# Splitting the inputs of the wide products two f-tiles at a time, with the combinations spread evenly: a packed attention and two feed-forward layers on one Trainium2 core

## The chip, the core and the metric

The kernel runs on one core of one Trainium2 chip, in one launch. The metric is the device time in microseconds. Engines are TensorE (PE; its weight loads are PEld), VectorE (DVE), ScalarE (ACT), GpSimd (POOL) and SyncE (SP), which issues the DMAs. Each engine works through its own queue in order, and semaphores order the engines among each other.

## What is computed

Attention in two hops gives x of 4608 rows and 512 columns; two feed-forward layers follow, each with a 512 x 2048 and a 2048 x 512 matrix:

```python
p_packed = sm_attn(p, k, v)                  # 32 packed rows per head
out = sm_attn(q, p_packed, p_packed)         # 8 x 8 heads, 576 rows, 64 columns
x = out.transpose(0, 2, 1, 3).reshape(4608, 512)
h = x @ w_in;  x = np.maximum(0.01 * h, h) @ w_out            # first layer
h = x @ w_in2; out = (h * (1 / (1 + np.exp(-1.702 * h)))) @ w_out2   # second layer
```

## The kernel before

There are four stages: attention with the first layer's narrow product (matmuls of L338), the first wide product 2048 to 512 (L650, into `y`), the second layer's first product (L684, into `h`), and the second wide product (L762, into `sum`).

Matrices are multiplied in about fp32 accuracy from fp32r parts: an operand a is split into a high part (a cast on ScalarE, `nc.scalar.copy`) and a low part (a minus the high part, a subtraction on VectorE), and each product is three matmuls: high with high, high with low, low with high. The helper `split(step, high)` puts the cast into the agenda of one step and the subtraction (L107, `tensor_sub(*rest)`) into that of the next. `side(step)` then emits what a step's agenda holds, in the order in which it was entered, ahead of that step's matmuls (in the middle stage behind them).

The two wide products work in a Strassen-Winograd scheme: a block of 768 rows is cut into two halves of rows i and two halves of the 2048 inputs h, and seven products (order 1, 7, 5, 6, 2, 4, 3) of eight f-tiles each replace eight. A block so has 56 steps (`steps`), and there are six blocks. A step of L650 is six matmuls of 384 columns, one of L762 nine of 256. The inputs of the products are the raw tiles a11, a12, a21, a22 (tags r.., two f-tiles, 128 x 2 x 384, in each) or combinations of them, made in place by VectorE in `prepare`'s `combo`: S3 (L480, a11-a21) is read by product 7, S1 (L482, a21+a22) by product 5, S2 (L484, a22-a11) by product 6, S4 (L486, a12-a11) by product 3. After S4 the raw tile a11 of the next block is loaded; a21, a22 and a12 of the next block are loaded during products 5, 4 and 3. Loads wait in SP's queue until the readers of the old tile are done.

`high` (L492) splits one f-tile of step k: its cast is in the agenda of step k-3, the subtraction in that of k-2, into one of five rotating buffers (`ROLL, LEAD = 5, 2`). The tiles are called `ba` in the first wide product (raw `br`) and `da` in the second (raw `dr`). The matmuls of step k read both parts, and free the buffer for step k+5.

Other work shares the queues. In L650, `combined("wi2", ...)` converts the second layer's weights from 64-bit words: per piece a load into `raw_wi`, two casts on ScalarE (L121, L122), on VectorE a mask (L125) and a shift-or (L128), an integer add on GpSimd (L129, `b_wi`), then four small subtractions on VectorE (L144 to L148) three steps later. A piece that is loaded in step s is cast in s+14; pieces start at steps 26 and 44 of the first block, at 1, 19 and 38 of the next four, and at 1 and 19 of the last. Finished products are copied or added out of PSUM by `evacuate` (ScalarE for products 1, 7, 2, VectorE for 5, 6, 4, 3).

`y_block` prepares the inputs of the middle stage: for each of seven products it casts (L586) and subtracts (L107, `ya`) the two 128 x 384 halves at steps of their own, and its `combo` (L592, L593, L595, L597 on tiles `yq`) follows the second half. It runs for block 0 in the second half of the last block of L650, for block 1 at the start of the middle stage, for the others within it. There the weights `wj` are split too (cast L626, subtraction L107), and `unit` takes the sums out (`uv`, `cc`, L688 to L703).

Of the kernel before, what the change touches and what calls it, by code (L numbers as in the profile page):

```python
# [9 lines left out]
F32 = mybir.dt.float32  # L10
F32R = mybir.dt.float32r
# [10 lines left out]
P = 128  # L22
# [4 lines left out]
HB = TB // 2  # L27
# [12 lines left out]
PLACE = {1: (0, 0), 7: (0, 0), 5: (1, 0), 6: (0, 0), 2: (0, 1), 4: (1, 1), 3: (0, 1)}  # L40

COMBO = {1: 0, 2: 1, 3: 2, 5: 3, 7: 4, 6: 5, 4: 6}
EARLY = 5
ROLL, LEAD = 5, 2


def packed_attention_moe_moe_kernel(tc, qT, kT, vm, vt, pT, w_in1, w_out1, w_in2, w_out2, out):
# [4 lines left out]
    nc = tc.nc  # L52
# [13 lines left out]
    pools = {}  # L66
# [13 lines left out]
    with ExitStack() as ctx:  # L80
# [10 lines left out]
        def at(step, *todo):  # L91
            agenda.setdefault(step, []).extend(todo)
# [9 lines left out]
        def split(step, high):  # L102


            rest = []
            at(step, lambda: rest.extend(high()))
            at(step + 1, lambda: nc.vector.tensor_sub(*rest))  # L107
# [299 lines left out]
        for c in range(1, 4):  # L407
            for k in range(4):
                s = 8 * c - 8 + k
# [4 lines left out]
        for b in range(B):  # L414
            s = 32 * b
# [18 lines left out]
        wt, raws, ga, outs, early = {}, {}, {}, {}, {}  # L434
# [39 lines left out]
        def prepare(nm, g):  # L474


            def combo(blk, fp, what):
                a11, a12, a21, a22 = (raws.get((blk, i, h, fp)) for i in range(2) for h in range(2))
                if what == "S3":
                    nc.vector.tensor_sub(a11, a11, a21)  # L480
                elif what == "S1":
                    nc.vector.tensor_add(a21, a21, a22)  # L482
                elif what == "S2":
                    nc.vector.tensor_sub(a11, a22, a11)  # L484
                else:
                    nc.vector.tensor_sub(a12, a12, a11)  # L486
                    load_raw(blk + 1, 0, 0, fp, nm, g)

            def high(k, blk, p, f):
                src = raws[(blk, *PLACE[p], f // 2)][:, f % 2, :]  # L490
                t = ga[blk, p, f] = pools["dr"].tile([P, 2, HB], F32R, tag=f"s{k % ROLL}", name=f"{nm}a_{blk}_{p}_{f}")
                nc.scalar.copy(t[:, 0, :], src)  # L492
                return t[:, 1, :], src, t[:, 0, :].bitcast(F32)

            for blk in range(NBK):
                s = 7 * NJ * blk
                for what, when in (("S3", (1, 4, 7, 10)), ("S1", (12, 14, 16, 19)), ("S2", (20, 22, 24, 27)), ("S4", (34, 38, 42, 46))):
                    for fp, k in enumerate(when):
                        at(s + k, lambda blk=blk, fp=fp, what=what: combo(blk, fp, what))
            for k, step in enumerate(steps):  # L500
                split(k - LEAD - 1, lambda k=k, step=step: high(k, *step))
                blk, p, f = step
                if f % 2 and p in (5, 4, 3):
                    at(k - LEAD, lambda blk=blk, p=p, f=f: load_raw(blk + 1, *PLACE[p], f // 2, nm, g))

        def evacuate(k, blk, p, bank, shape, store):
            def tile_(what):
# [62 lines left out]
        def y_block(early, steps, blk):  # L570
# [7 lines left out]
                    q[i, j] = pools[home].tile([P, 2, HB], F32, tag=tag, name=f"yq_{blk}_{i}{j}")  # L578
                    nc.sync.dma_start(q[i, j], yT[2 * j:2 * j + 2, :, t0 + HB * i:t0 + HB * i + HB].rearrange("d p t -> p d t"))

            def one(p, k):
                src, i = q[PLACE[p]], PRODUCTS.index(p)
                if blk not in ya:
                    ya[blk] = pools["ABC"[blk % 3]].tile([P, 7, 2, 2, HB], F32R, tag="ABC"[blk % 3], name=f"ya_{blk}")
                t = ya[blk][:, i]
                nc.scalar.copy(t[:, 0, k], src[:, k])  # L586
                return t[:, 1, k], src[:, k], t[:, 0, k].bitcast(F32)

            def combo(p):
                sub = nc.vector.tensor_sub  # L590
# [6 lines left out]
                    sub(q[0, 1], q[0, 1], q[0, 0])  # L597
            at(early, load)
            for n, step in enumerate(steps):
                p, k = (1, 2, 7, 5, 6, 4, 3)[n // 2], n % 2  # L600
                split(step, lambda p=p, k=k: one(p, k))
                if k:
                    at(step + 1, lambda p=p: combo(p))

        PIECES = (slice(0, 2), slice(2, 4), slice(4, 6), slice(6, 7))
# [117 lines left out]
        for q in range(2):  # L723
            s = 14 * NJ * q
# [87 lines left out]
```

## Time and profile before

| | |
|---|---|
| runs | 1481.79 us median of 3 (1481.16 to 1482.88) |
| profiled execution | 1488.2 us, of it the profile's span 1486.4 us |
| mean granted TensorE clock | 0.98 |
| TensorE, VectorE, ScalarE, GpSimd busy | 95%, 75%, 56%, 7% of the span |
| L650, first wide product | 367.05 to 751.36 us |
| L684, middle stage | 751.36 to 1117.18 us |
| L762, second wide product | 1117.18 us to the end |

Times in the profile are microseconds from the span's start. A bracket at the end of a row says how long the engine had stood idle before it, and what ended the idle time. A matmul is counted busy while it is in the pipeline, so TensorE counts as busy also where its matmuls are slower than they could be.

### The profile page before, as it was taken

The page shows a single profiled execution, that of the slowest core. Times are in us where ns is not written, and L with a number is a line of the kernel's source. Part 1 is how long each engine was busy: PE and PEld are TensorE (multiplying, and loading weights), DVE is VectorE, ACT ScalarE, POOL GpSimd, SP SyncE. Part 2 cuts the span into 40 slices and gives each one's busy share as a digit, 9 for nine tenths or more (in the row PEclk, how much of TensorE's full clock was granted, in tenths as well). Part 3 has the DMA queues.
Part 4 walks back from the last instruction along what each step waited for, and adds up shares of the span by engine and source line. Part 5 has one row for each costly group of instructions (what it writes and reads, how often), then busy time and mean ns, then how long its engine had stood idle before and what let it go on. Part 6 is the DMA issues. An engine that isn't in the chain of part 4 may idle for free.

```text
span 1486.4 us, 27714 instructions
## 1 busy us (share of the span) xinstructions
PE 1417.2 (95%) x10400; PEld 1322.9 (89%) x10400; DVE 1107.5 (75%) x2068; ACT 836.2 (56%) x1791; POOL 100.4 (7%) x71
## 2 busy tenths in 40 slices
PE   6789999999979999999889999999999999999998
PEld 4567777778979999999789999999999999999998
DVE  5667777762859888888987887877648877777776
ACT  3656666665435545555656766666645655445443
POOL 1311110100001010110100010000000000000000
PEclk8889999999989999999999999999999999999999
DMA  9459999969993655635357786786768524515421
GB/s 365 159 194 318 308 325 307 335 212 337 325 301 118 212 187 164 223 105 197 120 184 249 250 282 238 244 276 204 242 216 276 170 88 148 181 54 170 129 85 43
DMA packets 228773, 317.42 MB, mean 214 GB/s; under 512 B 12576, under 2 KB 188704, under 8 KB 228640
## 3 DMA queue, kind: packets, MB, share of 16 engines
q1 hardware_dynamic: 228640, 315.67, 63.9%
q8 instruction: 81, 1.33, 0.4%
q14 instruction: 52, 0.43, 0.1%
HBM read 191.89 MB, written 123.73 MB: 212 GB/s over the span
## 4 chain that ended last, share of the span: by engine, by line
PE 71%; DVE 17%; issue 4%; DMA 3%; ACT 2%; POOL 2%; SPq 1%; DVEq 0%; ACTq 0%; POOLq 0%
PE sum L762 23%; PE h L684 20%; PE y L650 14%; PE h L338 10%; DVE ba L107 3%; PE m L218 2%; POOL b_wi L129 1%; PE pp L273 1%; PE s L218 1%; DVE m L327 1%; DVE br L482 1%; DVE br L484 1%; DVE wj L107 1%; DVE ya L107 1%; DVE da L107 1%
## 5 line engine op out<-in xcount | busy, mean ns | idle before, releaser
L684 PE MATMUL h<-ya,wj 128*128 128x384 f32 x2016 | 357.7, 338 | 6.7 <-DVE uv L692 2.4
L684 PEld LDWEIGHTS h<-ya,wj 128*128 128x128 f32 x2016 | 352.5, 189 | 11.7 <-DVE uv L692 4.1
L338 PEld LDWEIGHTS h<-a,m 128*128 128x128 f32 x1536 | 215.7, 195 | 53.7 <-ACT g L343 22.1
L650 PE MATMUL y<-ba,wo 128*128 128x384 f32 x1296 | 238.1, 341 | 19.6 <-DVE ba L107 10.9
L650 PEld LDWEIGHTS y<-ba,wo 128*128 128x128 f32 x1296 | 225.6, 189 | 31.2 <-DVE ba L107 22.4
L492 ACT CAST ba<-br 128x384 fp32r<-128x384 f32 x336 | 164.5, 513 | 149.7 <-PE y L650 89.8
L338 PE MATMUL h<-a,m 128*128 128x288 f32 x1536 | 239.5, 309 | 9.3 <-ACT a L315 3.5
L492 ACT CAST da<-dr 128x384 fp32r<-128x384 f32 x336 | 166.3, 514 | 145.2 <-PE sum L762 105.4
L762 PE MATMUL sum<-wo,da 128*128 128x256 f32 x1944 | 232.4, 281 | 1.6 <-DVE da L107 1.4
L762 PEld LDWEIGHTS sum<-wo,da 128*128 128x128 f32 x1944 | 230.2, 188 | 3.2 <-DVE da L107 3.2
L107 DVE TENSOR_TENSOR da<-dr,da 128x384 fp32r<-128x384 f32 x336 | 172.8, 554 | 40.5 <-ACT da L492 40.4
L107 DVE TENSOR_TENSOR ba<-br,ba 128x384 fp32r<-128x384 f32 x336 | 175.7, 556 | 25.5 <-ACT ba L492 25.5
L343 ACT ACTIVATE g<-h 128x288 f32<-128x288 f32 x256 | 105.2, 416 | 99.7 <-PE h L338 98.0
L762 PE MATMUL sum<-wo_early,da 128*128 128x256 f32 x1080 | 132.4, 285 | 1.7 <-ACT da L492 1.6
L762 PEld LDWEIGHTS sum<-wo_early,da 128*128 128x128 f32 x1080 | 131.5, 193 | 2.2 <-ACT da L492 1.9
L650 PE MATMUL y<-ba,wo_early 128*128 128x384 f32 x720 | 128.2, 340 | 2.3 <-ACT ba L492 2.2
L650 PEld LDWEIGHTS y<-ba,wo_early 128*128 128x128 f32 x720 | 126.4, 190 | 3.3 <-ACT ba L492 2.4
L327 DVE TENSOR_TENSOR m<-m,m 128x512 fp32r<-128x512 f32 x64 | 43.0, 684 | 54.6 <-ACT m L325 54.2
L129 POOL TENSOR_TENSOR b_wo<-v_wo,b_wo 128x512 int32<-128x512 int32 x32 | 42.5, 1330 | 485.5 <-DVE v_wo L128 367.6
L677 ACT ACTIVATE g<-cc 128x384 f32<-128x384 f32 x96 | 50.4, 525 | 31.6 <-DVE cc L700 27.1
L107 DVE TENSOR_TENSOR wj<-wjs,wj 128x512 fp32r<-128x512 f32 x88 | 55.8, 647 | 9.7 <-ACT wj L626 9.7
L692 DVE TENSOR_TENSOR uv<-uv,h 128x384 f32<-128x384 f32 x48 | 26.5, 553 | 46.5 <-PE h L684 39.9
(114 smaller groups left out, 1372.1 us busy)
## 6 DMA issues: line engine op xcount, KB each, us to landing
g_scratch<-g SPq DMA_DIRECT2D x64, 576.0 KB, 5.3
br<-g_scratch SPq DMA_DIRECT2D x96, 384.0 KB, 7.0
g_scratch<-g SPq DMA_DIRECT2D x96, 384.0 KB, 5.4
dr<-g_scratch SPq DMA_DIRECT2D x96, 384.0 KB, 4.3
wjs<-wi_scratch SPq DMA_DIRECT2D x22, 896.0 KB, 5.8
wo_scratch<-hl_wo SPq DMA_DIRECT2D x32, 448.0 KB, 6.0
wo<-wo_scratch SPq DMA_DIRECT2D x27, 512.0 KB, 8.9
k<-in_kT_dram SPq DMA_DIRECT2D x16, 576.0 KB, 6.3
```

The source lines that it names most:

```text
L107: at(step + 1, lambda: nc.vector.tensor_sub(*rest))
L129: nc.gpsimd.tensor_tensor(d, v.bitcast(I32), d, op=ALU.add)
L218: nc.tensor.matmul(tiles[par][32 * i:32 * i + 32, :n], lhsT=lhsT(r, i, par), rhs=rhs(r, i), start=True, stop=True)
L327: nc.vector.tensor_sub(m[:, 1, par, :], t[par], m[:, 0, par, :].bitcast(F32))
L338: nc.tensor.matmul(t[:, :TH], lhsT=m[:, ws, par, o:o + P], rhs=a[:, xs, par, :], start=(k == 0), stop=(k == 5))
L343: nc.scalar.activation(g1t[g][:, f % 2, hf * TH:hf * TH + TH], t[:, :TH], AF.Prelu, alpha=0.01)
L492: nc.scalar.copy(t[:, 0, :], src)
L650: nc.tensor.matmul(acc[BANK[p]][:, c, :HB], lhsT=w[:, ws, P * c:P * c + P], rhs=x[:, xs, :], start=(p in OPENS and f + m == 0), stop=(f == ...
L677: nc.scalar.activation(g[f][:, HB * i:HB * i + HB], src, AF.Gelu_apprx_sigmoid)
L684: nc.tensor.matmul(b, lhsT=w[:, ws, c, P * kk:P * kk + P], rhs=x[:, xs, kk, :], start=(p in OPENS and kk + s == 0), stop=(kk + s == 3), sk ...
L692: nc.vector.tensor_add(v, v, b)
L762: nc.tensor.matmul(b, lhsT=x[:, xs, P * c:P * c + P], rhs=w[:, ws, :], start=(p in OPENS and f == 0 and m == 0 and c != 1), stop=(f == NJ ...
```

## The change

In the wide products one cast and one subtraction now serve the two f-tiles of a raw tile (128 x 768 columns); the cast stands in the agenda of step k-4 (k even), the subtraction in k-3, and there are three buffers of a pair each in place of five of one f-tile. The steps of the combinations are S3 1, 3, 5, 7 (before 1, 4, 7, 10), S1 9, 11, 13, 15 (12, 14, 16, 19), S2 17, 19, 21, 23 (20, 22, 24, 27) and S4 36, 39, 41, 43 (34, 38, 42, 46). The loads of the next block keep their steps, but for those that follow S4. In `y_block` a product's two halves are cast and subtracted together at the step of the first one, and the combination follows one step after.

```diff
-ROLL, LEAD = 5, 2
+ROLL = 3
...
             def high(k, blk, p, f):
-                src = raws[(blk, *PLACE[p], f // 2)][:, f % 2, :]
-                t = ga[blk, p, f] = pools["dr"].tile([P, 2, HB], F32R, tag=f"s{k % ROLL}", name=f"{nm}a_{blk}_{p}_{f}")
-                nc.scalar.copy(t[:, 0, :], src)
-                return t[:, 1, :], src, t[:, 0, :].bitcast(F32)
+                src = raws[(blk, *PLACE[p], f // 2)]
+                t = pools["dr"].tile([P, 2, 2, HB], F32R, tag=f"s{k // 2 % ROLL}", name=f"{nm}a_{blk}_{p}_{f}")
+                for c in range(2):
+                    ga[blk, p, f + c] = t[:, :, c]
+                nc.scalar.copy(t[:, 0], src)
+                return t[:, 1], src, t[:, 0].bitcast(F32)
...
-                for what, when in (("S3", (1, 4, 7, 10)), ("S1", (12, 14, 16, 19)), ("S2", (20, 22, 24, 27)), ("S4", (34, 38, 42, 46))):
+                for what, when in (("S3", (1, 3, 5, 7)), ("S1", (9, 11, 13, 15)), ("S2", (17, 19, 21, 23)), ("S4", (36, 39, 41, 43))):
...
             for k, step in enumerate(steps):
-                split(k - LEAD - 1, lambda k=k, step=step: high(k, *step))
                 blk, p, f = step
-                if f % 2 and p in (5, 4, 3):
-                    at(k - LEAD, lambda blk=blk, p=p, f=f: load_raw(blk + 1, *PLACE[p], f // 2, nm, g))
+                if f % 2 == 0:
+                    split(k - 4, lambda k=k, step=step: high(k, *step))
+                elif p in (5, 4, 3):
+                    at(k - 2, lambda blk=blk, p=p, f=f: load_raw(blk + 1, *PLACE[p], f // 2, nm, g))
...
-            def one(p, k):
+            def one(p):
...
-                nc.scalar.copy(t[:, 0, k], src[:, k])
-                return t[:, 1, k], src[:, k], t[:, 0, k].bitcast(F32)
+                nc.scalar.copy(t[:, 0], src)
+                return t[:, 1], src, t[:, 0].bitcast(F32)
...
             for n, step in enumerate(steps):
-                p, k = (1, 2, 7, 5, 6, 4, 3)[n // 2], n % 2
-                split(step, lambda p=p, k=k: one(p, k))
-                if k:
+                if n % 2 == 0:
+                    p = (1, 2, 7, 5, 6, 4, 3)[n // 2]
+                    split(step, lambda p=p: one(p))
                     at(step + 1, lambda p=p: combo(p))
```

## Rows read from the trace of the kernel before

**Rows 1.** The page's busy times: us, share of the span, instructions

```profile
PE 1417.2 (95%) x10400; PEld 1322.9 (89%) x10400; DVE 1107.5 (75%) x2068; ACT 836.2 (56%) x1791; POOL 100.4 (7%) x71
```

**Rows 2.** Busy us (instructions) by stretch: PE, PEld, DVE, ACT, POOL; granted clock; DMA

```profile
367.05:439.70 72.65, 63.41 (x338) 62.11 (x339) 48.81 (x85) 31.76 (x65) 1.43 (x1) 0.91 1.00 335
...
421.70:425.90 4.20, 1.44 (x3) 1.04 (x4) 2.57 (x5) 3.25 (x7) 0.03 (x1) 0.50 1.01 369
...
562.46:623.34 60.88, 59.68 (x338) 58.08 (x337) 51.99 (x95) 32.80 (x65) 6.26 (x3) 1.00 0.55 175
...
684.24:751.36 67.12, 61.81 (x338) 57.64 (x337) 62.13 (x113) 37.26 (x77) 5.70 (x2) 1.00 0.32 100
...
1117.18:1180.97 63.79, 62.33 (x505) 61.52 (x506) 56.27 (x96) 39.56 (x80) 0.00 (x0) 0.97 0.75 250
1180.97:1240.88 59.91, 59.87 (x507) 59.67 (x506) 45.53 (x77) 29.85 (x59) 0.00 (x0) 1.00 0.42 133
```

**Rows 3.** The chain that ended last, in L650: start us, us, what

```profile
451.96 0.94 DVE ba L107 x2
452.90 0.87 DVE br L482
...
546.69 32.39 PE y L650 x185
```

**Rows 4.** Groups of instructions by form: busy us, mean ns, idle before

```profile
L107 DVE TENSOR_TENSOR ba<-br,ba 128x384 fp32r<-128x384 f32 x336 | 175.7, 556 | 25.5 <-ACT ba L492 25.5
...
L492 ACT CAST ba<-br 128x384 fp32r<-128x384 f32 x336 | 164.5, 513 | 149.7 <-PE y L650 89.8 <-DVE br L482 25.0 <-DVE br L484 21.1
...
L155 ACT CAST hl_wo<-b_wo 128x896 fp32r<-128x896 f32 x16 | 15.1, 945 | 8.9 <-DVE b_wo L148 8.6 <-issue 0.3
...
L315 ACT CAST a<-a 128x576 fp32r<-128x576 f32 x16 | 10.8, 674 | 7.6 <-DVE a L313 7.6
...
L128 DVE SCALAR_TENSOR_TENSOR v_wi<-v_wi,raw_wi 128x512 uint32<-128x512 uint32 x16 | 11.0, 685 | 0.0
...
L125 DVE TENSOR_SCALAR raw_wi<-raw_wi 128x512 uint32<-128x512 uint32 x16 | 6.8, 425 | 12.4 <-ACT v_wi L122 11.3 <-DMA br<-g_scratch 1.1
...
L513 ACT COPY v<-y 128x768 f32<-128x768 f32 x6 | 4.8, 798 | 2.5 <-PE y L650 2.5
...
L148 DVE TENSOR_TENSOR b_wi<-b_wi 128x128 f32<-128x128 f32 x16 | 4.7, 292 | 0.6
```

**Rows 5.** Timeline of VectorE and GpSimd in L650's fourth block: start us, us, what

```profile
581.89 2.05 DVE L482 TENSOR_TENSOR br<-br,br 128x768 f32<-128x768 f32 x1
...
603.22 3.29 POOL L129 TENSOR_TENSOR b_wi<-v_wi,b_wi 128x512 int32<-128x512 int32 x1 [20.10 <-DVE v_wi L128]
...
606.54 0.29 DVE L144 TENSOR_TENSOR b_wi<-b_wi 128x128 f32<-128x128 f32 x1 [1.18 <-POOL b_wi L129]
```

**Rows 6.** Timeline of TensorE in the same block

```profile
607.56 4.65 PE L650 MATMUL y<-ba,wo 128*128 128x384 f32 x25 [0.46 <-DVE ba L107]
```

**Rows 7.** Timeline of ScalarE and TensorE at the stop in the first block

```profile
422.09 0.66 ACT L121 ACTIVATE b_wi<-raw_wi 128x512 int32<-128x512 uint32 x1 [9.50 <-DMA raw_wi<-in_w_in_dram]
...
423.75 0.69 PE L650 MATMUL y<-ba,wo 128*128 128x384 f32 x1 [8.25 <-ACT ba L492]
```

**Rows 8.** Timeline of TensorE in the last block of L650

```profile
744.96 6.36 PE L650 MATMUL y<-ba,wo 128*128 128x384 f32 x35 [1.36 <-DVE ba L107]
```

**Rows 9.** Timeline of VectorE and TensorE at the start of L684

```profile
760.44 1.29 DVE L107 TENSOR_TENSOR wj<-wj 128x512 fp32r<-128x512 f32 x2
...
761.78 12.44 PE L684 MATMUL h<-ya,wj 128*128 128x384 f32 x68 [0.19 <-DVE wj L107]
...
762.23 0.96 DVE L592 TENSOR_TENSOR yq<-yq,yq 128x768 f32<-128x768 f32 x1
```

**Rows 10.** Timeline of VectorE and TensorE in L684, near 926 us

```profile
925.47 0.96 DVE L592 TENSOR_TENSOR yq<-yq,yq 128x768 f32<-128x768 f32 x1
...
928.87 73.90 PE L684 MATMUL h<-ya,wj 128*128 128x384 f32 x420 [1.46 <-DVE uv L692]
```

## The prediction

> **What bounds the kernel now.** I first read the busy shares of the page [rows 1]: TensorE is busy 95% of the span, so a change to the preparing engines can win only the time in which matmuls stand still. Where that is, the table of stretches tells, cut at the end of each block of the first wide product (L650), and then at the second (L762) [rows 2]. One unbroken piece of the chain, 185 matmuls in 32.39 us [rows 3], gives 0.175 us a matmul, 1.05 us a step of six, 58.8 us a block of 56 steps. The six blocks take 72.65, 61.76, 61.00, 60.88, 60.90 and 67.12 us (rows stand for the first, the fourth and the last): over 58.8 they lose 13.8, 2.9, 2.2, 2.1, 2.1 and 8.3, together 31 us. The first block of L762 takes 63.79 us where a later one takes 59.91, and VectorE has room in the later one (45.5 us busy of 59.9): there is nothing to win in the last five blocks. So the change lives on the 31 us, some 4 us of L762's first block, and whatever it does to the middle stage (L684).
>
> What causes the loss in a usual block: VectorE is busy 52.0 of 60.9 us, and its work is bunched. Matmuls break in two places, inside product 5 and at the start of product 4 (for which the row stands), each time waiting for VectorE's low part (`ba L107`) [rows 6]. In the first, a combination took 2.05 us instead of 0.95 because GpSimd's integer add was running; in the second, that add was itself stretched to 3.29 us, and VectorE stood 1.18 us waiting for it with low parts queued behind [rows 5]. A few waits of 0.3 to 0.5 us, plus the late weight load behind each, make the 2.1 us.
>
> **The change, part by part.** *Casts.* One 128x384 cast takes 513 ns; forms of 576 and 896 columns take 674 and 945 [rows 4], so 768 is near 0.84 us (674 + 192 x 271/320 = 837 ns), against two of 513. ScalarE is busy 32.8 of 60.9 us: the saving is worth nothing in itself, but the first high part now comes 0.32 us later.
>
> *Low parts.* A single subtraction is 556 ns, but two in a row take 0.94 us in the chain and one of 768 columns in a row takes 0.87 [rows 3, 4]. A pair saves 0.07 us of a busy VectorE, 28 x 0.07 = 2 us a block. The bounds are 0.07 and, if the two stand apart and each pays its full length, 2 x 0.556 - 0.95 = 0.16 us. I take 0.07, because the places that hurt are those where VectorE runs without gaps. The Trainium skill (VectorE: DVE Perf Modes, section "The DRAIN you can't avoid") says a VectorE instruction cannot start until the one ahead has emptied the pipe, so that each instruction left out saves its fixed part: by it a pair saves 0.16 us and a block 4.4 us, and the forecast below would be about 1 us lower. The trace does not agree, since two subtractions in a row take 0.94 and not 1.11 us.
>
> *Lead.* With three pair buffers the cast of step k (even) may begin when step k-5 has ended, that is at the start of k-4. Cast 0.84 plus subtraction 0.95 is 1.8 us, and the pair is due at k, 4.2 us later: 2.4 us in hand. Before, five buffers gave the same start for each step, 0.51 + 0.55 us of work and 3.1 us in hand. So the margin shrinks by 0.7 us. Against that the combinations move: they now come one every two steps, some three steps ahead of the cast that reads them, where before the last ones (steps 19, 24, 27) shared or nearly shared the step of their cast.
>
> *Steps 15 to 26 of a usual block, laid out.* Each two steps (2.1 us) VectorE has a combination and a low part, 2 x 0.87 = 1.74 us, so 0.36 us is spare. The conversion's instructions are 0.43, 0.69 and four of 0.29 us [rows 4]; in a row each shows 0.09 less (0.556 against 0.47), so 0.34 + 0.6 + about 0.95 with small gaps. With one collision of 1.1 us (2.05 - 0.95) that is 3.0 us. Four spare gaps take 1.4 us, so low parts fall 1.6 us behind, within the 2.4 in hand, and after step 24 there are no combinations. The copy of product 7 (0.80 us [rows 4]) stands ahead of one cast in ScalarE's queue and takes some 0.6 us of that, which brings the tightest pair (steps 24 to 26) to about 0.2 us before it is due. At step 42 the same count with the 1.18 us wait leaves 0.6 us. I take 0.5 us left of each block's loss (0 to 1.2). Gain: 2.4 us in the second block and 3 x 1.6 = 4.8 in the next three.
>
> *First block.* Its 13.8 us are mostly one stop: a weight conversion's cast (L121) waits in ScalarE's queue until 422 us for its load, and TensorE idles 8.25 us [rows 7]; the granted clock stands at 0.50 there, that is 1.2 GHz, and at a mean of 0.91 in the block [rows 2]. The loads that stand ahead of it in SP's queue are the same after, so the load lands at the same time. But the cast of steps 44 and 45 is now queued in step 40 ahead of L121, where before only that of 43 was: TensorE runs two steps (2.1 us) further. When the load lands, VectorE has the shift-or (0.6), one combination (0.87) and a 0.95 us low part before the next pair is whole, about 1 us more than now. Gain 1.1 us (0 if that pair's cast is late too; 2.1 if the next pair comes no later than now). The block's start loses: the first cast is 0.32 us longer and its low part 0.4, so 0.7 us. A stop in product 6 gives back 0.4. Together +0.8.
>
> *Last block.* Here blocks of y are split besides, and VectorE is the bound: it is busy 62.1 us of 67.1 [rows 2], and TensorE stops for 1.4 us at a time (three stops of 1.1 to 1.4; the row is the last) for `ba L107` [rows 8]. Adding up the second half from step 24 (14 pairs of low parts 12.2 us, 7 of y 6.1, eight combinations 7.0, sums 3.5, weights 2.1, conversion 1.9, one wait 1.2) gives some 34 us for 29.4, with 2.4 in hand; laid out, three stops of 3.2, 0.2 and 1.1 us remain. Loss 4.5 (3 to 7) instead of 8.3: gain 3.8.
>
> *Middle stage.* Blocks of y also move: the combinations follow the first pair's low part at once. At the stage's start this is against the change. Today the weights' low parts (760.44, two of them) come ahead of the combinations (762.23), and TensorE waits for the weights until 761.78 [rows 9]. After, the longer cast of y stands ahead of the weights' casts (+0.4 us) and the two combinations (1.74 us) ahead of their subtractions: up to 2.4 us more. But VectorE runs without gaps there until 777 us, and a later stop shrinks by most of it. I take a loss of 1.0 (2.4 to -0.5). Near 926 us it is for the change: the two combinations, 0.96 us each, stand ahead of `uv L692`, for which TensorE waits 1.46 us [rows 10]; they move four steps forward, to where VectorE waits for a load. Gain 1.0 (0 to 2). Sum 0.
>
> *Second wide product.* Its start loses 0.7 us like the first's. Its first block loses 63.79 - 59.91 = 3.9 us [rows 2], a good part of it to the clock at the start (mean 0.97); of the rest I take 1.0 back. Sum +0.3.
>
> **The sum.** 0.8 + 2.4 + 4.8 + 3.8 + 0 + 0.3 = 12.1 us off a profiled execution of 1488.2 us (span 1486.4 and 1.8 around it): 1476.1. The runs' median is 1481.79, 6.4 us under the profiled one, so 1481.8 - 12.1 = 1470.
>
> **The rivals.** *GpSimd waits longer.* The 16 conversions each need GpSimd's add, and VectorE waits three steps later. Its add was held up while four VectorE instructions ran back to back [rows 5]; instructions of 0.87 us leave it fewer openings than those of 0.47. If the add is always late, ten more waits of 1.18 us fall on VectorE, 12 us, of which the margin hides about half: gain 12 - 6 = 6, some 1476. For it: the margin at step 42 is 0.6 us. Against: with one combination in two steps VectorE has a gap in each pair. The Trainium skill (SBUF — State Buffer, section "Who interferes with whom") has a rule for it: of a VectorE instruction with two SBUF inputs and a GpSimd one that reads SBUF, the later is held until the earlier ends. By that rule the trace agrees, in both directions (2.05 and 3.29 us). Chance 0.17.
>
> *The loss only moves.* VectorE's work falls by 2 us of 52 a block; if spacing does nothing and only this counts, 0.07 x 28 is won where VectorE is the bound (about half of each of six blocks, 6 us), and the 2.4 us in the middle stage and two starts (1.4) are lost: gain about 2, 1480. Against: the stops sit where work is bunched. Chance 0.14.
>
> *Three buffers are too few (slower).* The place is the copy of a finished sum, 0.8 us on ScalarE ahead of a cast: the margin is then 1.7 us. If VectorE is more than 1.7 us behind whenever it comes, each time costs 0.5 us; three times a block over twelve blocks is 18 us, more than the 12 won: 1488. Against: in later blocks of L762 VectorE is busy 76%. Chance 0.07.
>
> **How the numbers follow.** The forecast has 0.62: 1470, its own range 1464 to 1476 from the bounds above. The range 1463 to 1480 adds the two smaller gains and leaves out the slower case. A measurement tells about 0.2%, 3 us: under 1478.8 is faster. The first two cases and little of the third: faster 0.81, same 0.12, slower 0.07.
>
> **What would show it.** Blocks two to five of L650 near 59.3 us, with no stop in product 5; the stop before 424 us about 2 us shorter at its front end; the last block near 63; L684's start 1 to 2 us worse and no stop at 929 us; the later blocks of L762 unchanged at 60. Wrong if those last blocks grow (buffers), if stops for `ba` remain in products 5 and 4 (GpSimd), or if L121's load lands at another time.

## The result and the profile after

The kernel after takes 1471.62 us (median of six runs, 1468.14 to 1475.48) beside 1485.19 us for the kernel before (six runs, 1481.16 to 1489.58): a ratio of 0.9909, 95% interval 0.9882 to 0.9937. The profiled execution takes 1473.39 us (span 1471.6) where that of before took 1488.2 (span 1486.4), so the two traces hold 14.8 us of difference. Lines below the edits have moved: L653 is the first wide product, L687 the middle stage, L765 the second wide product, L494 the cast, L595, L596, L598 and L600 the combinations of y; the combinations of the wide products keep L480 to L486.

The page of the kernel after, busy times, against [rows 1]: VectorE and ScalarE run 378 instructions fewer each, and VectorE is busy only 14 us less.

```profile
PE 1409.1 (96%) x10400; PEld 1325.2 (90%) x10400; DVE 1093.6 (74%) x1690; ACT 784.7 (53%) x1413; POOL 97.4 (7%) x71
```

The table by stretch of the kernel after, cut as [rows 2] (busy us of PE, PEld, DVE, ACT, POOL, granted clock, DMA share, GB/s): first block of L653, its fourth, its last; the start of L687 and its rest; the first and the second block of L765.

```profile
368.15:441.39 73.24, 63.48 (x336) 62.51 (x337) 48.34 (x56) 27.23 (x34) 1.82 (x1) 0.91 0.99 334
...
559.30:617.74 58.44, 58.44 (x338) 58.21 (x337) 51.67 (x68) 28.98 (x37) 5.65 (x4) 1.00 0.58 187
...
676.17:740.85 64.68, 60.00 (x337) 58.00 (x337) 60.18 (x79) 33.00 (x44) 6.75 (x3) 1.00 0.34 108
740.85:769.63 28.78, 23.99 (x123) 22.39 (x122) 21.19 (x32) 16.87 (x30) 1.29 (x1) 0.94 0.60 216
769.63:1105.96 336.33, 332.33 (x1895) 330.49 (x1895) 247.27 (x464) 208.04 (x430) 19.68 (x15) 1.00 0.73 245
1105.96:1167.49 61.53, 61.33 (x505) 61.04 (x505) 55.15 (x68) 35.45 (x50) 0.00 (x0) 0.97 0.77 257
1167.49:1227.50 60.01, 60.01 (x506) 60.01 (x505) 44.71 (x49) 25.50 (x31) 0.00 (x0) 1.00 0.42 132
```

The usual blocks (the second is 59.48 us, the third to fifth 58.43 or 58.44) are where the time came from. The first block is longer than before, and so is L687's start; L687's rest is 3.5 us shorter (336.33; before 339.80). L687's start in the kernel before:

```profile
751.36:777.38 26.02, 22.46 (x122) 20.48 (x120) 21.58 (x38) 17.32 (x37) 1.26 (x1) 1.00 0.68 248
```

Of the 2.8 us more that it takes after, TensorE stands still for 1.2 and its matmuls take 1.5 (23.99 for 22.46), at a granted clock of 0.94 in place of 1.00.

TensorE in the fourth and the last block, against [rows 6, 8], then GpSimd and VectorE in the last. The fourth runs unbroken from end to end; the last keeps stops, one of them (3.23 us) longer than any it had before (1.43), behind an add of 3.63 us.

```profile
559.30 20.97 PE L653 MATMUL y<-ba,wo_early 128*128 128x384 f32 x120
580.11 37.79 PE L653 MATMUL y<-ba,wo 128*128 128x384 f32 x216
...
717.78 3.63 POOL L129 TENSOR_TENSOR b_wi<-v_wi,b_wi 128x512 int32<-128x512 int32 x1 [19.62 <-DVE v_wi L128]
...
720.29 1.94 DVE L598 TENSOR_TENSOR yq<-yq,yq 128x768 f32<-128x768 f32 x1
...
725.02 4.63 PE L653 MATMUL y<-ba,wo 128*128 128x384 f32 x24 [3.23 <-DVE ba L107]
730.50 10.51 PE L653 MATMUL y<-ba,wo 128*128 128x384 f32 x59 [0.85 <-DVE ba L107]
```

VectorE and GpSimd in the fourth block, against [rows 5]:

```profile
574.99 0.96 DVE L107 TENSOR_TENSOR ba<-br,ba 128x768 fp32r<-128x768 f32 x1 [0.26 <-ACT ba L494]
...
579.41 1.89 POOL L129 TENSOR_TENSOR b_wi<-v_wi,b_wi 128x512 int32<-128x512 int32 x1 [18.88 <-DVE v_wi L128]
...
580.07 2.05 DVE L107 TENSOR_TENSOR ba<-br,ba 128x768 fp32r<-128x768 f32 x1
582.04 0.28 DVE L144 TENSOR_TENSOR b_wi<-b_wi 128x128 f32<-128x128 f32 x1
```

The collisions are still there: this low part takes 2.05 us beside the add. But VectorE had stood waiting for a cast shortly before (0.26 us here), so it was ahead of its work, the late pair is not yet due, and no matmul stops. A usual block's three adds take 1.88 to 1.90 us each, where before two took 1.48 or 1.49 and one 3.29, and L144 no longer waits for them.

The stop in the first block, ScalarE, VectorE, GpSimd and TensorE, against [rows 7]:

```profile
423.69 0.66 ACT L121 ACTIVATE b_wi<-raw_wi 128x512 int32<-128x512 uint32 x1 [9.31 <-DMA raw_wi<-in_w_in_dram]
...
425.67 0.69 PE L653 MATMUL y<-ba,wo 128*128 128x384 f32 x1 [6.62 <-ACT ba L494]
426.00 0.95 DVE L486 TENSOR_TENSOR br<-br,br 128x768 f32<-128x768 f32 x1
426.26 1.82 POOL L129 TENSOR_TENSOR b_wi<-v_wi,b_wi 128x512 int32<-128x512 int32 x1 [106.53 <-DVE v_wi L128]
426.87 2.89 DVE L107 TENSOR_TENSOR ba<-br,ba 128x768 fp32r<-128x768 f32 x2
...
428.95 12.61 PE L653 MATMUL y<-ba,wo 128*128 128x384 f32 x59 [2.58 <-DVE ba L107]
```

The weights' load lands 1.6 us later than before and TensorE's first stop is 1.6 us shorter. Then two low parts, 1.82 us together elsewhere in this trace, take 2.89 beside the add, and a second stop of 2.58 us follows.

The start of L687, against [rows 9]: the combinations L595 and L596 now stand ahead of the weights' low parts, and TensorE waits 2.58 us for these.

```profile
750.60 0.96 DVE L595 TENSOR_TENSOR yq<-yq,yq 128x768 f32<-128x768 f32 x1
751.60 0.96 DVE L596 TENSOR_TENSOR yq<-yq,yq 128x768 f32<-128x768 f32 x1
...
752.93 1.62 DVE L107 TENSOR_TENSOR wj<-wj 128x512 fp32r<-128x512 f32 x3
...
754.27 14.34 PE L687 MATMUL h<-ya,wj 128*128 128x384 f32 x71 [2.58 <-DVE wj L107]
```

### The profile page after: what moved, and what is told of

Read it like the earlier page. It is cut to its first block, busy times and chain, and to the rows that moved or that the text cites. A ratio compares the mean times of both kernels' runs of the same rounds, so it can differ in the third digit from the quotient of the medians.

```text
span 1471.6 us, 26611 instructions
## 1 busy us (share of the span) xinstructions
PE 1409.1 (96%) x10400; PEld 1325.2 (90%) x10400; DVE 1093.6 (74%) x1690; ACT 784.7 (53%) x1413; POOL 97.4 (7%) x71
## 5 line engine op out<-in xcount | busy, mean ns | idle before, releaser
L687 PE MATMUL h<-ya,wj 128*128 128x384 f32 x2016 | 356.3, 338 | 6.9 <-DVE wj L107 2.6
L687 PEld LDWEIGHTS h<-ya,wj 128*128 128x128 f32 x2016 | 353.0, 189 | 10.0 <-DVE wj L107 3.7
L338 PEld LDWEIGHTS h<-a,m 128*128 128x128 f32 x1536 | 216.0, 195 | 53.3 <-ACT g L343 22.1
L653 PE MATMUL y<-ba,wo 128*128 128x384 f32 x1296 | 231.6, 339 | 14.2 <-DVE ba L107 7.6
L653 PEld LDWEIGHTS y<-ba,wo 128*128 128x128 f32 x1296 | 226.8, 189 | 18.1 <-DVE ba L107 11.1
L494 ACT CAST da<-dr 128x768 fp32r<-128x768 f32 x168 | 140.2, 836 | 171.4 <-PE sum L765 155.5
L765 PE MATMUL sum<-wo,da 128*128 128x256 f32 x1944 | 230.4, 280 | 0.0
L765 PEld LDWEIGHTS sum<-wo,da 128*128 128x128 f32 x1944 | 229.8, 188 | 0.0
L494 ACT CAST ba<-br 128x768 fp32r<-128x768 f32 x168 | 140.5, 837 | 165.1 <-PE y L653 120.6
L107 DVE TENSOR_TENSOR da<-dr,da 128x768 fp32r<-128x768 f32 x168 | 160.6, 956 | 75.2 <-ACT da L494 74.2
L107 DVE TENSOR_TENSOR ba<-br,ba 128x768 fp32r<-128x768 f32 x168 | 170.3, 1019 | 44.3 <-ACT ba L494 43.9
L765 PE MATMUL sum<-wo_early,da 128*128 128x256 f32 x1080 | 132.2, 285 | 2.1 <-ACT da L494 1.9
L765 PEld LDWEIGHTS sum<-wo_early,da 128*128 128x128 f32 x1080 | 131.3, 192 | 2.7 <-ACT da L494 2.2
L653 PE MATMUL y<-ba,wo_early 128*128 128x384 f32 x720 | 128.3, 340 | 3.3 <-ACT ba L494 2.7
L653 PEld LDWEIGHTS y<-ba,wo_early 128*128 128x128 f32 x720 | 126.6, 190 | 4.2 <-ACT ba L494 2.9
L107 DVE TENSOR_TENSOR wj<-wjs,wj 128x512 fp32r<-128x512 f32 x88 | 55.6, 646 | 7.5 <-ACT wj L629 7.4
```

The lines of the kernel that those rows point to most:

```text
L338: nc.tensor.matmul(t[:, :TH], lhsT=m[:, ws, par, o:o + P], rhs=a[:, xs, par, :], start=(k == 0), stop=(k == 5))
L494: nc.scalar.copy(t[:, 0], src)
L653: nc.tensor.matmul(acc[BANK[p]][:, c, :HB], lhsT=w[:, ws, P * c:P * c + P], rhs=x[:, xs, :], start=(p in OPENS and f + m == 0), stop=(f == ...
L687: nc.tensor.matmul(b, lhsT=w[:, ws, c, P * kk:P * kk + P], rhs=x[:, xs, kk, :], start=(p in OPENS and kk + s == 0), stop=(kk + s == 3), sk ...
L765: nc.tensor.matmul(b, lhsT=x[:, xs, P * c:P * c + P], rhs=w[:, ws, :], start=(p in OPENS and f == 0 and m == 0 and c != 1), stop=(f == NJ ...
```

## The experiments

A *usual block* below is the time from one block's first matmul to the next one's in TensorE's timeline, for the fourth block of the first wide product if nothing else is said. The kernel before has 60.88 us there and the kernel after 58.44.

**1. The new steps alone**, single f-tiles and five buffers kept:

```diff
-("S3", (1, 4, 7, 10)), ("S1", (12, 14, 16, 19)), ("S2", (20, 22, 24, 27)), ("S4", (34, 38, 42, 46))
+("S3", (1, 3, 5, 7)), ("S1", (9, 11, 13, 15)), ("S2", (17, 19, 21, 23)), ("S4", (36, 39, 41, 43))
```

> The kernel before with the new steps of the combinations alone (S3 1,3,5,7; S1 9,11,13,15; S2 17,19,21,23; S4 36,39,41,43); one f-tile to a cast and five buffers as before. Theory A, the loss of the usual blocks of L650 comes from VectorE's combinations being bunched with its low parts: the third to fifth blocks fall from 60.9 to 58.4 to 59.2 us, and the ratio to before is 0.991 to 0.994. Theory B, it comes from the number of VectorE's and ScalarE's instructions: those blocks stay above 60.3 us, and the ratio is 0.998 to 1.001.

Measured: ratio 0.9985 (0.9970 to 1.0000), a usual block of 60.75 us. In that block VectorE shows one wait of 0.34 us between 565 and 595 us and is otherwise busy throughout. Its timeline and those of GpSimd and TensorE:

```profile
584.44 2.05 DVE L484 TENSOR_TENSOR br<-br,br 128x768 f32<-128x768 f32 x1
...
585.61 23.20 PE L650 MATMUL y<-ba,wo 128*128 128x384 f32 x127
...
604.06 3.29 POOL L129 TENSOR_TENSOR b_wi<-v_wi,b_wi 128x512 int32<-128x512 int32 x1 [18.39 <-ACT ba L492]
...
607.38 0.29 DVE L144 TENSOR_TENSOR b_wi<-b_wi 128x128 f32<-128x128 f32 x1 [1.18 <-POOL b_wi L129]
...
609.27 15.96 PE L650 MATMUL y<-ba,wo 128*128 128x384 f32 x89 [0.46 <-DVE ba L107]
```

The 2.05 us collision, the 3.29 us add and VectorE's wait of 1.18 us for it are as in [rows 5]. From the first of the 127 matmuls to the end of the stop behind them 23.66 us pass, where 127 x 0.174 = 22.1. These are the values of theory B: spacing does not suffice in the first wide product. In the second, where GpSimd adds nothing, it takes the three stops out (0.48, 0.27 and 0.62 us): behind the first 180 matmuls the first block takes 38.83 us, before 40.26. The block as a whole falls further, from 63.79 to 60.88 us, but the other half of that is the clock: those 180 matmuls take 22.05 us at a granted clock of 1.00, before 23.53 at 0.93, and the kernel of experiment 4, with the old steps there, has the same 22.04 at 1.00.

**2. The pairs alone**, with three buffers, y as before and the old steps, but for S1's last sum (18 in place of 19) and S2's last (26 in place of 27), which a pair needs earlier:

```diff
-ROLL, LEAD = 5, 2
+ROLL = 3
...
+                t = pools["dr"].tile([P, 2, 2, HB], F32R, tag=f"s{k // 2 % ROLL}", name=f"{nm}a_{blk}_{p}_{f}")
...
+                if f % 2 == 0:
+                    split(k - 4, lambda k=k, step=step: high(k, *step))
```

> The kernel before with casts and subtractions of two f-tiles and three pair buffers in the wide products, but the old steps of the combinations, but for the last S1 (18 in place of 19) and the last S2 (26 in place of 27), which a pair's cast would otherwise overtake. Blocks of y as before. Theory A: the third to fifth blocks of L650 stay above 60.0 us, ratio 0.996 to 1.000. Theory B: they fall to 58.4 to 59.2 us, ratio 0.991 to 0.994.

Measured: ratio 1.0334 (1.0312 to 1.0355), a usual block of 65.34 us, which neither theory foresaw. So half of the change costs 3.3%, the other half wins almost nothing, and together they win 0.9%: neither count nor spacing alone is the cause.

**3 and 4. The y blocks apart.** The third kernel is the one after with y's halves split one at a time as before, the fourth the one before with y in pairs:

```diff
...
-                if n % 2 == 0:
-                    p = (1, 2, 7, 5, 6, 4, 3)[n // 2]
-                    split(step, lambda p=p: one(p))
+                p, k = (1, 2, 7, 5, 6, 4, 3)[n // 2], n % 2
+                split(step, lambda p=p, k=k: one(p, k))
+                if k:
```

> The changed kernel with blocks of y split by halves as before (the wide products changed in full). If the pairs of y cost the start of L684 and give back later in it, as the two traces say: that start falls from 28.8 back to about 26 us, the rest of the stage rises from 336.3 to 339 to 340 us, and the sum is within 1.5 us of the changed kernel, ratio to before 0.990 to 0.993. If the later gain in L684 came from elsewhere (the timing with which the stage is entered), the rest stays near 336 and the ratio is 0.989 or less. The last block of L650 should rise from 64.7 by up to 1 us.

> The kernel before with the pairs of y alone. Usual blocks of L650 unchanged at 60.9 us; the start of L684 2 to 3 us longer than before (26.0), the rest of the stage 3 to 4 us shorter than before (339.8), the last block of L650 within 1 us of 67.1: ratio 0.998 to 1.001. If the start's loss belongs to the wide products instead, it stays at 26 us and the ratio is about 0.997.

Measured: ratios 0.9897 (0.9873 to 0.9921) and 0.9979 (0.9964 to 0.9994). With halves, L687's start is 26.4 us and its rest 338.8; with pairs in the old kernel 28.7 and 336.4. The y pairs move some 2.5 us from the rest to the start and win next to nothing: with halves in the new kernel the ratio is no worse, and of the little that pairs win in the old kernel, 1.5 us lie in the trace in the first 180 matmuls of L762, which the edit does not touch. The gain is all in the inputs of the wide products.

**5. The combinations of y one step later** in the kernel after:

```diff
-                    at(step + 1, lambda p=p: combo(p))
+                    at(step + 2, lambda p=p: combo(p))
```

> The kernel after, with the combination of the y halves one step later than its pair's split. In the kernel after the start of L687 is 28.8 us against 26.0 before, and two combinations (L595, L596) stand on VectorE ahead of the first weight subtraction; the rest of the stage is 3.5 us shorter than before, which came from the y pairs (the run with split halves lost it again). Theory: the start is worse because of the early combinations, the later gain comes from the pairs themselves, so the start falls to 26 to 27 us while the rest stays near 336.3, and the whole is 2 to 2.5 us below the kernel after (near 1469). Rival: the later gain comes from the early combinations, so the rest goes back to 338 to 339 and the whole stays within 0.7 us of the kernel after. Second rival: the start is longer because a pair's first cast and subtraction are twice as long, not because of the combinations, so the start stays at 28 to 29 and so does the whole.

Measured: ratio 0.9891 (0.9867 to 0.9916); start 25.6 us, rest 338.55, as in the first rival. The timeline of VectorE, ScalarE and TensorE near 912 us shows what gave the gain back:

```profile
907.99 0.95 DVE L595 TENSOR_TENSOR yq<-yq,yq 128x768 f32<-128x768 f32 x1
...
908.97 0.96 DVE L596 TENSOR_TENSOR yq<-yq,yq 128x768 f32<-128x768 f32 x1
...
910.45 0.55 DVE L703 TENSOR_TENSOR cc<-uv,h 128x384 f32<-128x384 f32 x1
...
911.03 0.52 ACT L680 ACTIVATE g<-cc 128x384 f32<-128x384 f32 x1 [2.35 <-DVE cc L703]
...
911.46 0.46 ACT L691 COPY uv<-h 128x384 f32<-128x384 f32 x1
...
911.98 1.33 PE L687 MATMUL h<-ya,wj 128*128 128x384 f32 x6 [1.93 <-ACT uv L691]
```

At the start TensorE waits 0.60 us for the weights' low part, not 2.58. But near 908 us the combinations of a later y block now stand ahead of L703; the gelu that reads its result stands on ScalarE ahead of `uv L691`, for which TensorE waits 1.93 us. The whole, 1469.22 us, is 2.4 us under the kernel after, but in the trace 2.1 of this are in the first block of L653 (71.17 us), which the edit does not touch.

**6. The first piece of the second layer's weights later** in the kernel after:

```diff
-        combined("wi2", [26, 44] + [56 * blk + k for blk in range(1, 5) for k in (1, 19, 38)] + [281, 299], 14)
+        combined("wi2", range(44, 44 + 16 * 17, 17), 14)
```

> The kernel after, with the sixteen pieces of the second layer's weights spread evenly from step 44 (every 17 steps) instead of a first one at step 26. In the kernel after the first block takes 73.2 us where the others take 58.4; ScalarE waits 9.3 us at L121 for the load of that first piece, and casts of the products stand behind it. Theory: that one wait makes 6.6 + 2.6 us of TensorE's stops in the first block, so the block falls to 63 to 66 us, no L121 wait over 2 us is left in it, and the whole is 7 to 10 us below the kernel after (1462 to 1465), the other blocks within 0.5 us of 58.4. Rival: the load is late because the first block's own loads share its queues, and the next wait (for a raw tile of the second block, or a piece's load) takes the place of this one; then the stop moves to the end of the block or into the second, blocks one and two together fall by less than 3 us.

Measured: ratio 0.9827 (0.9806 to 0.9848), 1461.01 us; the first block takes 62.57 us, the next four 58.94, 58.78, 58.69 and 58.56. TensorE in the first block has no stop after its start:

```profile
366.82 24.03 PE L653 MATMUL y<-ba,wo_early 128*128 128x384 f32 x119 [0.55 <-DVE ba L107]
390.69 37.87 PE L653 MATMUL y<-ba,wo 128*128 128x384 f32 x216
```

Beside the kernel after the block is 10.7 us shorter and the whole 10.6, some three quarters of what the change itself won. This is more than the wait: the edit moves the piece's whole conversion out of the block, its add included. Both stops go with it (6.62 and 2.58 us), and the matmuls behind them, 59 in 12.44 us at a granted clock of 0.82 in the kernel after, run at 1.00.

**7, 8 and 9. Without GpSimd's add**, in the kernel before, in that of experiment 1, and in the kernel after. The edit is the same in all three, and `add` is false for the pieces of `wi2`:

```diff
...
-            nc.gpsimd.tensor_tensor(d, v.bitcast(I32), d, op=ALU.add)
+            if add:
+                nc.gpsimd.tensor_tensor(d, v.bitcast(I32), d, op=ALU.add)
```

> The kernel before, without GpSimd's integer add in the conversion of the second layer's weights (so these lack the added high word; nothing else is left out). It tells what the collisions of GpSimd and VectorE are worth with single f-tiles and the old steps. Theory (an interaction: with single f-tiles VectorE's work from step 1 to 28 of a block has no slack, so anything that lengthens it stops TensorE): without the add the usual blocks fall from 60.9 to 59 to 59.7 us, five of them 6 to 9 us, as the burst of casts and combinations still stands. Rival 1, collisions alone are the loss: 58.4 to 58.7 us each, 11 to 12 us in all. Rival 2, collisions cost nothing and the count and order of VectorE's instructions alone make the loss: 60.5 to 60.9 us, under 2 us in all.

> The kernel before with the new steps of the combinations alone, without GpSimd's integer add in the conversion of the second layer's weights (so these lack the added high word; nothing else is left out). With the add this kernel's usual blocks took 60.75 us and VectorE ran without a gap for 30 us of each. Theory: the new steps and the freed VectorE time are needed together; the add's collisions are worth about 3 us of VectorE time per block, so without it the new steps are enough and the usual blocks fall to 58.4 to 59.0 us, lower than the kernel before without the add. Rival: single f-tiles are too many instructions whatever else runs (the pairs' own saving is what counts): 60 us and more, as with the add.

> The kernel after without GpSimd's integer add in the conversion of the second layer's weights (so these lack the added high word; nothing else is left out). It tells what the collisions of GpSimd and VectorE still cost after the change. Theory: nothing in the usual blocks, since VectorE now has slack there (58.4 us as with the add), 1 to 2 us in the first block (after its stop a low part met the add and the next stop of 2.6 us stood behind it: 73.2 to 71 to 72), 2.5 to 3.5 us in the last (64.7 to 61 to 62); in all 4 to 6 us below the kernel after. Rival: collisions cost nothing after the change, and the first and last block keep their times within 0.5 us.

Measured: the kernel before 0.9932 (0.9913 to 0.9952), usual block 59.02 us; with the new steps 0.9891 (0.9871 to 0.9912), 58.77 us; the kernel after 0.9847 (0.9824 to 0.9870), 58.27 us. The usual block in the table by stretch, columns as above, first of the kernel before without the add:

```profile
553.58:612.60 59.02, 58.70 (x338) 58.18 (x338) 50.84 (x95) 32.80 (x65) 0.00 (x0) 1.00 0.59 187
```

With the new steps:

```profile
554.80:613.57 58.77, 58.56 (x337) 58.24 (x337) 50.91 (x95) 33.47 (x65) 0.00 (x0) 1.00 0.57 184
```

The kernel after:

```profile
553.64:611.91 58.27, 58.27 (x337) 58.27 (x337) 49.63 (x68) 28.98 (x37) 0.00 (x0) 1.00 0.57 189
```

The add costs a usual block 60.88 - 59.02 = 1.86 us with single f-tiles and old steps, 60.75 - 58.77 = 1.98 with the new steps, and 58.44 - 58.27 = 0.17 in the kernel after. Of the 2.44 us that the change wins in a usual block, 1.69 are what the add no longer costs; the other 0.75 (59.02 to 58.27) are won without any add. VectorE's own work, read here where nothing stretches it, falls from 50.9 to 49.6 us a block, 1.2 to 1.3 us for 28 pairs. In the kernel after the first block falls to 69.91 us (the two stops are 4.99 and 1.52 us) and the last to 62.39: more than expected in the first, a little less in the last.

**10. A shorter lead** in the kernel after:

```diff
-("S3", (1, 3, 5, 7)), ("S1", (9, 11, 13, 15)), ("S2", (17, 19, 21, 23))
+("S3", (3, 5, 7, 9)), ("S1", (11, 13, 15, 17)), ("S2", (19, 21, 23, 25))
```

> The kernel after with S3, S1 and S2 two steps later (3, 5, 7, 9; 11, 13, 15, 17; 19, 21, 23, 25), so that a sum stands one step ahead of the cast that reads it instead of three. Theory: the pairs lost 3.3% with the old steps because a pair's cast there waited for its sum, and the next sum for the cast (2.80 us for a pair in series where TensorE takes 2.1); with one step of lead most of that series is back in products 7, 5 and 6, so the usual blocks rise from 58.4 to 59.5 to 62 us, with stops of 0.2 to 0.6 us at each pair. Rival: what hurt the pairs alone was that the old steps put the sums late and unevenly, not their distance from the cast; then even spacing at any lead is enough and the blocks stay within 0.3 us of 58.4.

Measured: ratio 0.9899 (0.9878 to 0.9920); the usual block takes 58.96 us with one stop, which falls between the two expectations, 0.5 us under the first and 0.2 beyond the second:

```profile
580.15 8.82 PE L653 MATMUL y<-ba,wo 128*128 128x384 f32 x49
589.22 29.25 PE L653 MATMUL y<-ba,wo 128*128 128x384 f32 x167 [0.25 <-DVE ba L107]
```

So two of the three steps of lead are worth 0.5 us a block, and the 65 us of the pairs alone need another reason. In experiment 2 the sums of products 5 and 6 follow each other at the same distance as here, but each one step later, in the very step of its cast.

**11. The pairs alone, without the add:**

> The kernel before with pairs and three buffers alone (old steps, so that the sums of products 5 and 6 stand in the very step of the cast that reads them), without GpSimd's integer add in the conversion of the second layer's weights (these lack the added high word; nothing else is left out). With the add its usual blocks took 65.3 us. Since a lead of one step cost the kernel after only 0.54 us a block, the distance alone does not explain 65.3. Theory: a sum in the cast's own step puts sum, cast and low part in series (2.80 us a pair where TensorE takes 2.1), collisions or not, so without the add the usual blocks still take 63.5 to 65.3 us. Rival: the collisions with the add use up the buffers and make the series; without it 58.3 to 60 us, as in the other three kernels without the add.

Measured: ratio 1.0317 (1.0285 to 1.0349), usual block 65.32 us, with or without the add. ScalarE and VectorE in the middle of product 7:

```profile
580.43 0.95 DVE L483 TENSOR_TENSOR br<-br,br 128x768 f32<-128x768 f32 x1
...
581.49 0.83 ACT L495 CAST ba<-br 128x768 fp32r<-128x768 f32 x1 [1.97 <-PE y L654]
...
582.36 0.96 DVE L107 TENSOR_TENSOR ba<-br,ba 128x768 fp32r<-128x768 f32 x1 [0.98 <-ACT ba L495]
583.24 0.95 DVE L483 TENSOR_TENSOR br<-br,br 128x768 f32<-128x768 f32 x1
...
584.30 0.84 ACT L495 CAST ba<-br 128x768 fp32r<-128x768 f32 x1 [1.97 <-DVE br L483]
...
585.17 0.96 DVE L107 TENSOR_TENSOR ba<-br,ba 128x768 fp32r<-128x768 f32 x1 [0.98 <-ACT ba L495]
```

Sum (L483), cast (L495), low part (L107), and only then the next sum, which stands behind that low part in VectorE's queue: 2.81 us a pair (583.24 - 580.43) where TensorE takes 2.08. VectorE idles 0.98 us of each, the cast 1.97. Both engines have time, and neither may use it.

**12. Three moves together** in the kernel after:

```diff
-        combined("wi2", [26, 44] + [56 * blk + k for blk in range(1, 5) for k in (1, 19, 38)] + [281, 299], 14)
+        combined("wi2", range(44, 44 + 16 * 15, 15), 14)
...
-                    at(step + 1, lambda p=p: combo(p))
+                    at(step + (2 if early < 0 else 1), lambda p=p: combo(p))
```

> The kernel after with three things moved: the pieces of the second layer's weights start at step 44 and follow every 15 steps, so that the last is converted at the start of the last block; the combinations of the y halves are one step later in the first y block of L687 alone, the later ones as in the kernel after. Theory: the first block falls to 62 to 63 us as with pieces every 17 steps; the last block's stop of 3.2 us came from a piece's GpSimd add beside a combination of y and is gone, so that block takes 61 to 62 us where it took 64.7; the start of L687 takes 25.6 us where it took 28.8, and the rest stays near 336.3, since the stop at 912 us of the run with all combinations later came from the later blocks of y. Together 16 to 17 us below the kernel after, near 1455. Rivals: the start's gain goes back later whatever the later combinations do (rest 339, the whole near 1458); the stop in the last block is the combination's own length and not the add's, so that block stays near 65 (near 1459).

Measured: 1457.45 us, ratio 0.9792 (0.9768 to 0.9816), the lowest median of all, though its interval touches that of experiment 6. The first block takes 61.80 us and the last 60.67, a little better than expected; L687's start takes 26.41, 0.8 more (at a granted clock of 0.94, in experiment 5 1.00), and its rest 336.56, so this time the gain does not go back. What is missing to 1455 is in the blocks between (59.42, 58.74, 60.34 and 59.73 us): every 15 steps a piece falls on other steps of each block, and some of these stop TensorE for 0.2 to 0.4 us.

## Why the prediction was right, and where its sizes were off

The forecast was 1470 us in 1463 to 1480, the measurement 1471.62, and the 12.1 us of the sum stand against 14.8 between the two traces and 13.6 between the medians. That 1470 came so close is in part luck: the base of 1481.79 us was the median of three runs, three later ones of the same kernel took 1487.50 to 1489.58, so the base was 3.4 us too low, and the gain, put too low as well, makes up for part of that. Within the sum, too, errors of both signs cancel. The mechanism of the likeliest case holds as far as that the usual blocks lost their stops; what took the stops away is only in part what the prediction says. By terms:

| term | predicted us | measured us |
|---|---|---|
| before L653 starts (367.05, 368.15) | 0 | -1.1 |
| first block | +0.8 | -0.6 |
| second block | +2.4 | +2.3 |
| third to fifth block | +4.8 | +7.5 |
| last block | +3.8 | +2.4 |
| L687: start, rest | -1.0, +1.0 | -2.8, +3.5 |
| L765: first block, rest | +0.3 | +2.3, +1.3 |

*Usual blocks.* Two sizes were off in the same direction. The floor was taken as 58.8 us from a piece of 185 matmuls; a clean block is 58.4 (58.27 without the add), 0.174 us a matmul. And 0.5 us of each block's loss was to stay, counted from a conversion in which the collision comes once and the wait of 1.18 us again at step 42; nothing stayed. In the step that laid out steps 15 to 26 the pair of steps 24 to 26 had 0.2 us in hand; the trace shows no stop there, with a collision of 1.1 us in place.

*What the gain is made of.* The prediction put it on the bunching, and that alone is not it: with single f-tiles the new steps win 0.1 us a block. The runs show that pairs and steps only work together, and the traces three things in that. The pairs free 1.2 to 1.3 us of VectorE a block; I had 28 x 0.07 = 2.0. The even steps put that freed time ahead of the collisions: this is read from VectorE's waits, four of 0.17 to 0.29 us between 569 and 578 us in the kernel after, where the new steps alone have one of 0.34 us in 30, and no run tests it by itself. And the lead keeps a pair's sum out of the step of its cast; without it the pairs lose 4.5 us a block. With all three the add's collisions, of 1.1 us each, cost a block 0.17 us, in the kernel before and with the new steps alone some 1.9.

*GpSimd waits longer* (0.17) came out for two of a block's three adds (1.48 to 1.9 us), but the one for which VectorE had waited fell from 3.29 to 1.9, and the waits of VectorE on which that rival rests did not come. The Trainium skill (SBUF — State Buffer, section "Who interferes with whom") has the later of the two held until the earlier ends, and the rows agree: the add that starts at 579.41 ends at 581.30, and the low part that starts at 580.07 ends at 582.12, 0.82 us later, close to its own length. *The loss only moves* fell with the unbroken blocks, *three buffers are too few* with later blocks of L765 that stay at 60.0.

*First block.* The front of the stop came out nearly as predicted (TensorE's wait 8.25 to 6.62 us, with a load that landed 1.6 us later, 1.1 of it with the whole product). The step that failed is the next pair "about 1 us more than now": the two low parts behind the stop took 2.89 us beside the add, and a stop of 2.58 us followed. Without the add that stop is 1.52 us, and the block 69.91 us; part of that is the first stop, which is 1.6 us shorter there for a reason that the runs don't show. The term itself is hardly measured: experiments 3 and 5 leave this block as in the kernel after, and it takes 72.76 and 71.17 us there (stops of 6.23 and 5.52), experiment 4 leaves it as before and has 72.37; the -0.6 lies within that. The -1.1 ahead of it is no better known: no experiment changes the stage before, and the first matmul of the wide product comes between 363.12 and 368.20 us in them.

*Last block.* The stops were to be 3.2, 0.2 and 1.1 us; they are 3.23 and 0.85 us, with 0.36 and 0.24 ahead of them. The block takes 64.68 us where the term made it 63.3. The 3.23 us stop is the add's doing in part, as I had not seen: it started at 717.78 and ended 3.63 us later, and the combination behind it (L598) took 1.94 us. Without the add the stop is 2.22 us, so a third of it is the add's. With the last piece converted at the block's start, ahead of the y work, no stop is over 1.2 us, and the block takes 60.67.

*L687.* The two signs were right and both sizes too small; the sum is within 0.7 us of the 0 that was predicted. At the start the stops cost 1.2 us more, close to the 1.0 of the term; what it lacked is the 1.5 us of slower matmuls at a granted clock of 0.94. The five traces with the stop of 2.58 us have 0.88 to 0.94 there and experiments 3 and 5 have 1.00, but experiment 12 has 0.94 without that stop, so what lowers the clock stays open. Each half is due to the y pairs alone (experiments 3 and 4), and moving the combinations brings the one back for the other, unless only the first block's are moved (experiment 12).

*L765.* I gave 0.3 us to a block that lost 3.9, a good part of which I put down to the clock. That reading was right: the first 180 matmuls take 23.53 us before and 23.51 after, at a granted clock of 0.93, where a later block's take 21.58 at 1.00. The term for the rest was too small: the other 324 matmuls fell from 40.26 to 38.02 us, so 2.2 us came back and not 1.0. The start loses 0.5 us of waits (1.92 and 0.20 us, before 1.60), 0.3 of them ahead of the block's first matmul. The new steps alone bring 1.4 of the 2.2. The 1.3 us in the later blocks were not foreseen; the runs don't show what made them.

## What to carry to other kernels

Where one engine prepares the next one's inputs in a chain (sum, cast, low part), a link that stands in the same step as its reader puts the whole chain in series through the queue, however much time each engine has; one step of lead removes nearly all of it (65.3 to 58.96 us a block). Judge a change of such a schedule by the stretch in which an engine has no gap: the same collision costs 1.9 us a block where VectorE has none, and 0.2 us where it waits for 0.2 or 0.3 us at a time. And first look for the longest single wait: here one early load (9.3 us of wait at L121) with the conversion behind it was worth some 9 to 11 us in its block, for one changed list of steps.

## What the runs showed of the hardware

A merged VectorE subtraction saves little: two low parts of 768 columns in a row take 1.82 us and start 0.87 apart, two of 384 take 0.94, and over a block's 28 pairs the busy time that nothing stretches falls by 1.2 to 1.3 us, 0.05 us each. By the Trainium skill (VectorE: DVE Perf Modes, section "The DRAIN you can't avoid") the prediction worked out 0.16 us each, which is 4.5 us a block and not the 4.4 given there. The section adds that a next instruction that is not held starts earlier. The rows agree with that: subtractions of 384 columns in a row start 0.47 us apart, where one alone takes 0.556.

VectorE's busy time hardly fell in a usual block (51.99 us of 60.88 before, 51.67 of 58.44 after), because a held instruction counts as busy: what it does when nothing holds it is 50.84 and 49.63 us. The busy row so hides the half of the change that the runs without the add make visible.
